# The soft threshold of the later batches on ScalarE and GpSimd instead of VectorE

## The chip, the cores and the metric

The kernel runs on one core of a Trainium2 chip. The metric is the device time of one execution in microseconds (us). Engines are named as in the profile: PE is TensorE's matmul stream and PEld its weight loads, DVE is VectorE, ACT is ScalarE, POOL is GpSimd, SP is the engine that issues most DMAs.

## The reference, cut to what matters

```python
batch, seq, dim = (8, 3008, 256)
X = np.fft.rfft(x, axis=1)
Yr = Xr @ w_r - Xi @ w_i + b_r
Yi = Xr @ w_i + Xi @ w_r + b_i
lam = 0.01
Yr = np.sign(Yr) * np.maximum(np.abs(Yr) - lam, 0.0)
Yi = np.sign(Yi) * np.maximum(np.abs(Yi) - lam, 0.0)
y = np.fft.irfft(Yr + 1j * Yi, n=seq, axis=1)          # (8, 3008, 256)
h = y.reshape(24064, 256) @ w_in                       # w_in: 256 x 2048
out = np.maximum(h, 0.0) ** 2 @ w_out                  # w_out: 2048 x 256
```

Each batch goes through a Fourier transform along the sequence, a complex linear layer, a soft threshold with lam = 0.01, the inverse transform, and a two-layer network with a squared relu.

## The kernel before, in words

**The network** is nearly all of the PE's work. A tile of 500 or 504 tokens (six tiles a batch, 48 in all) meets 8 blocks of the hidden layer; each meeting is a `Step`. Its first layer is made of seven products in PSUM tiles `psh` (left factor `win`, right factor `yt`), three matmuls each, since every number is carried as a high and a low part. DVE adds them up and takes the relu (`mp`, `mu`, `mv`, `mc`), ACT squares `mc` and rounds the square to its high part `mg`, POOL subtracts to get the low part, also `mg`, and 12 matmuls into `pso` (with `wout`) follow two half steps later. A step is done in two slots of the main loop, so a batch has 96 slots. The helper `then` (L486) fixes the order of these instructions on each engine.

**The transform** of the next batch is done beside it. This text calls that a round: in round 1 the network works on the first batch and the transform of the second is made, and so on to round 7, which makes the eighth batch. (The first batch's own transform comes before all that, in a front part of some 150 us with another code, `Unit32`, which the change leaves alone.) In a round, the 24 groups of frequencies are worked off as 12 pairs, `Pair`. A pair runs through these methods: `fwd` makes the second half of the transform (L284, into a PSUM tile `psf`); ACT copies a part (`kq`) and rounds (`kxh`), DVE subtracts (`kxl`) and adds (`kp`); `sums` rounds `kp` on ACT and subtracts on POOL (`kxl` again); `mix` makes two of the three products of the complex layer (L305, 12 matmuls into one `psf`), and DVE adds the bias (`ke`, L317). `shrink` makes the third product (L305, 6 matmuls into another `psf`), DVE combines all in four additions of 64 partitions (`kv`, L326), and then comes the threshold: v minus v clipped to plus or minus lam (L328, L329). ACT rounds the result to `ksh`, POOL subtracts to `ksl`. `back` (L337) runs the inverse, six matmuls for each group of the pair into one `psf` each, four with `ksh` and two with `ksl` in a pair; ACT rounds the outcome (`kuh`), DVE subtracts (`kul`), and both go out by DMA. Other users of `psf` are `Fwd.run` (L240, read by ACT into `xe`) and `Back.mm` (L465 to L469, read by ACT into `dy` and by DVE into `yr`). `Tokens` makes the next tile's `yt` on ACT and POOL from `yr` and `ms`.

All `psf` tiles share two banks of PSUM, in turn: the tile after next has to wait until the bank's readers are done.

**What sets the order.** The main loop emits the methods by due times (in `pair_tasks`, for example, `shrink` comes 4.0 slots after `fwd`, and `back(0)` 7.1 slots after it). A scheduler, which runs a timeline of its own when the kernel is built, then orders all instructions on each engine; at run time each engine takes its own in that order, and an instruction that waits holds up those behind it.

## Time and profile before

| | |
|---|---|
| median of 3 runs | 2633.39 us (2633.01 to 2635.26) |
| profiled execution | 2629.59 us |
| its span, first to last instruction | 2627.5 us |
| PE, DVE, ACT, POOL busy in it | 98%, 68%, 50%, 63% |
| granted TensorE clock | 0.994 |

PE is nearly always busy, so what matters is the small rest: where PE waits, and for whom. Rounds 2 to 6 look alike in the trace, each about 318 us long.

### The profile page before, as it was taken

How to read it: one execution, taken by the hardware profiler on the slowest of the kernel's cores; microseconds unless marked ns; L12 is line 12 of the kernel's file. 1: busy time of each engine (PE TensorE's matmuls, PEld its weight loads, DVE VectorE, ACT ScalarE, POOL GpSimd, SP SyncE). 2: the span in 40 equal slices, each digit the busy share in tenths (PEclk: the TensorE clock that was granted, in tenths of full speed). 3: DMA queues.
4: the chain of work that ended last, by engine and by line, in shares of the span. 5: the costliest groups of instructions: out<-in, count | busy, mean ns of one | idle time of the engine just before them, and what ended most of it. 6: DMA issues, size and time to landing. Idle time of an engine off the chain costs nothing.

```text
span 2627.5 us, 47126 instructions
## 1 busy us (share of the span) xinstructions
PE 2568.5 (98%) x16908; PEld 2348.4 (89%) x16908; DVE 1775.4 (68%) x3797; ACT 1305.1 (50%) x2050; POOL 1655.1 (63%) x1635
## 2 busy tenths in 40 slices
PE   6899999999999999999999999999999999999999
PEld 4789989999899998999989998999989999899998
DVE  7887775666766767566676666666666677665554
ACT  3555445454554545545545444555445454445443
POOL 2356667666766667667666676676667665666564
PEclk8999999999999999999999999999999999999999
DMA  8733333233332333233332333323332222211000
GB/s 267 248 105 107 94 115 93 87 104 103 93 89 88 102 103 87 89 106 98 99 92 81 100 101 104 99 76 98 104 104 83 69 85 80 83 57 47 27 29 16
DMA packets 191066, 250.47 MB, mean 95 GB/s; under 512 B 21790, under 2 KB 135958, under 8 KB 190834
## 3 DMA queue, kind: packets, MB, share of 16 engines
q1 hardware_dynamic: 177970, 223.40, 27.7%
q0 software_dynamic: 12864, 24.07, 4.1%
q8 instruction: 135, 2.21, 0.4%
q14 instruction: 97, 0.79, 0.1%
HBM read 146.85 MB, written 100.53 MB: 94 GB/s over the span
## 4 chain that ended last, share of the span: by engine, by line
PE 88%; DVE 5%; DMA 2%; POOL 2%; issue 1%; ACT 0%; SPq 0%; POOLq 0%; DVEq 0%; ACTq 0%
PE pso L488 38%; PE psh L488 34%; PE psf L305 6%; PE psf L284 2%; PE psf L240 2%; PE psf L337 2%; PE psf L468 1%; PE psf L469 1%; DMA xt<-x_in 1%; PE psf L465 1%; POOL mg L105 1%; DVE kc L328 1%; DVE kv L105 0%; DMA s<-xe 0%; DMA x<-x_in 0%
## 5 line engine op out<-in xcount | busy, mean ns | idle before, releaser
L105 POOL TENSOR_TENSOR mg<-mc,mg 128x500 fp32r<-128x500 f32 (+1 forms) x768 | 965.0, 1277 | 602.6 <-ACT mg L98 542.2
L488 PE MATMUL pso<-mg,wout 128*128 128x500 f32 (+1 forms) x4608 | 1159.4, 392 | 0.4 <-ACT mg L98 0.2
L488 PE MATMUL psh<-yt,win 128*128 128x250 f32 (+1 forms) x8064 | 1077.6, 281 | 3.2 <-DVE mc L102 3.2
L488 PEld LDWEIGHTS psh<-yt,win 128*128 128x128 f32 x8064 | 1020.8, 189 | 33.1 <-PE psh L488 2.7
L488 PEld LDWEIGHTS pso<-mg,wout 128*128 128x128 f32 x4608 | 826.2, 189 | 135.0 <-ACT mg L98 0.7
L102 DVE CUSTOM_DVE_ANT_0 mc<-psh,mv 128x500 f32<-128x500 f32 (+3 forms) x768 | 419.2, 548 | 412.6 <-PE psh L488 370.0
L488 ACT ACTIVATE mc<-mc 128x1000 f32<-128x1000 f32 (+1 forms) x384 | 400.8, 1044 | 478.3 <-DVE mc L102 477.3
L98 ACT CAST mg<-mc 128x1000 fp32r<-128x1000 f32 (+1 forms) x384 | 396.8, 1033 | 18.5 <-ACT mc L488 0.4
L488 DVE TENSOR_TENSOR mv<-psh,mu 128x500 f32<-128x500 f32 (+1 forms) x384 | 260.6, 679 | 51.4 <-PE psh L488 19.3
L305 PE MATMUL psf<-wx,kxh 128*128 128x256 f32 x1008 | 207.5, 282 | 2.7 <-ACT xe L98 1.3
L99 DVE COPY mp<-psh 128x250 f32<-128x250 f32 (+1 forms) x384 | 160.1, 417 | 48.9 <-PE psh L488 27.1
L326 DVE TENSOR_TENSOR kv<-psf,ke 64x256 f32<-64x256 f32 x336 | 141.9, 422 | 57.6 <-PE psf L305 50.3
L305 PEld LDWEIGHTS psf<-wx,kxh 128*128 128x128 f32 x1008 | 165.3, 188 | 6.4 <-ACT xe L98 1.5
L488 DVE TENSOR_TENSOR mu<-psh,mp 128x250 f32<-128x250 f32 (+1 forms) x384 | 160.6, 418 | 11.2
L105 POOL TENSOR_TENSOR ksl<-kv,ksh 128x512 fp32r<-128x512 f32 x84 | 108.7, 1295 | 89.3 <-ACT ksh L98 88.5
L102 DVE CUSTOM_DVE_ANT_0 mc<-psh,mp 128x250 f32<-128x250 f32 (+1 forms) x384 | 157.2, 409 | 1.8 <-PE psh L488 1.4
L98 ACT COPY dy<-psf 128x188 f32<-128x188 f32 x256 | 77.0, 314 | 151.0 <-PE psf L469 149.9
L219 POOL TENSOR_TENSOR xs<-xt 120x256 f32<-120x256 f32 x156 | 116.5, 764 | 50.4 <-DMA xt<-x_in 38.5
L305 PE MATMUL psf<-wx,kxl 128*128 128x256 f32 x504 | 141.1, 280 | 3.5 <-POOL kxl L105 2.8
L98 ACT CAST kuh<-psf 128x256 fp32r<-128x256 f32 x192 | 68.2, 372 | 124.2 <-PE psf L337 107.6
L475 DVE TENSOR_TENSOR yr<-psf,dy 128x188 f32<-128x188 f32 (+4 forms) x256 | 78.3, 313 | 74.5 <-ACT dy L98 68.4
L317 DVE TENSOR_TENSOR ke<-psf,bias 128x512 f32<-128x512 f32 x84 | 58.1, 692 | 100.8 <-PE psf L305 100.3
(103 smaller groups left out, 2531.4 us busy)
## 6 DMA issues: line engine op xcount, KB each, us to landing
du<-s SPq DMA_DIRECT2D x128, 256.0 KB, 2.9
s<-kuh SPq DMA_DIRECT2D x192, 128.0 KB, 2.1
s<-kul SPq DMA_DIRECT2D x192, 128.0 KB, 2.6
ka<-s SPq DMA_DIRECT2D x84, 256.0 KB, 3.4
kcm<-cm_in POOLq DMA_DIRECT2D x84, 256.0 KB, 3.5
s<-xe SPq DMA_DIRECT2D x85, 240.0 KB, 2.4
xt<-x_in SPq DMA_DIRECT2D x84, 240.0 KB, 3.5
du<-s SPq DMA_DIRECT2D x256, 64.0 KB, 2.8
```

The costliest lines, as they stand in the source:

```text
L98: return act.copy(out=out, in_=in_)
L99: return eng.tensor_copy(out=out, in_=in_)
L102: return dve._custom_dve(TENSOR_ADD_SAT, out=out, in0=in0, in1=in1, s0=_float(0x7F7FFFFF), s1=0.0)
L105: return eng.tensor_tensor(out=out, in0=a, in1=b, op=ALU.subtract)
L219: return eng.tensor_tensor(out=out[:, :n], in0=self.xt[:, :n, 0], in1=self.xt[:, :n, 1], op=(ALU.add, ALU.subtract)[t])
L240: nc.tensor.matmul(ps[:M1, t], am32[:, t], self.u[:, t], start=True, stop=True)
L284: nc.tensor.matmul(pv[:, :, c, g, :], self.a[:, g, c * 128:(c + 1) * 128], bg, start=True, stop=True)
L305: self.last = nc.tensor.matmul(ps, l, wx[j][:, k, c, :], start=n == 0, stop=n == 5)
L317: dve.tensor_add(out=self.e, in0=self.pe, in1=bias)
L326: dve.tensor_add(out=v[64 * r:64 * r + 64, g], in0=ps[gs], in1=self.e[gs, r])
L475: self.cut = dve.tensor_add(out=o, in0=ps[:, 0, lo:hi], in1=y[:, c, lo:hi])
L488: last_of[eng] = op(*args, **kwargs)
```

## The change

The threshold of `Pair.shrink` is made as relu(v - lam) - relu(-v - lam). Both relus run on ACT (with a bias that is read from a small tile `low`, filled once with -lam), the subtraction runs on POOL. The clip and the subtraction on DVE go. It concerns 84 pairs, 12 in each of 7 rounds.

```diff
@@ fnet_moe
+    low = const.tile([128, 1], F32, name="low")
...
     nc.sync.dma_start(am32, a32)
+    dve.memset(low, -LAM)
@@ Pair.shrink
                 for r in range(2):
                     dve.tensor_add(out=v[64 * r:64 * r + 64, g], in0=ps[gs], in1=self.e[gs, r])
-            cl = T("kc", [128, 2, D], F32, tag="ke")
-            dve.tensor_scalar(out=cl, in0=v, scalar1=-LAM, scalar2=LAM, op0=ALU.max, op1=ALU.min)
-            sub(dve, v, v, cl)
+            r = T("kc", [128, 2, D], F32, tag="ke")
+            act.activation(r, v, AF.Relu, bias=low)
+            act.activation(v, v, AF.Relu, bias=low, scale=-1.0)
+            sub(pool, v, r, v)
             self.sh = T("ksh", [128, 2, D], F32R)
             self.sl = T("ksl", [128, 2, D], F32R)
             halves(self.sh, self.sl, v, pool)
```

Since the scheduler orders everything anew, the change also moves instructions that the diff does not touch. Up to the first pair of round 1 the order is the same; from there it differs on every engine. Rounds 4 and 6 of the new order are alike, and nearly like round 2; rounds 3 and 5 are alike. Three places show what moved. In the changed kernel a line's number is 1 to 3 higher than before (L284 is L286, L305 is L307, L337 is L340, L488 is L491).

**Place 1: PE, the ninth pair of a round.** Before, in round 4, the first half of this pair's `back` stands inside a run of `pso` matmuls:

```order
L488 MATMUL pso_15737<-mg_16062,wout_83 128x500
L488 MATMUL pso_15737<-mg_16062,wout_84 128x500
L337 MATMUL psf<-ksh,kcm 128x256 x2
L337 MATMUL psf<-ksl,kcm 128x256
L488 MATMUL pso_15738<-mg_16062,wout_83 128x500
L488 MATMUL pso_15738<-mg_16062,wout_84 128x500
```

Now, in the same round:

```order
L468 MATMUL psf<-dx_sb,du 128x2x94
L471 MATMUL psf<-dx_sb,du 128x2x94
L472 MATMUL psf<-dx_sb,du 128x188
L491 MATMUL psh_16286<-yt_16019,win_81 128x250
L286 MATMUL psf<-kb,ka 128x2x64 x4
L340 MATMUL psf<-ksh,kcm 128x256 x4
L491 MATMUL psh_16286<-yt_16018,win_81 128x250
L491 MATMUL psh_16286<-yt_16018,win_82 128x250
L340 MATMUL psf<-ksl,kcm 128x256 x2
L307 MATMUL psf<-wx_79,kxh 128x256
L307 MATMUL psf<-wx_79,kxl 128x256
```

Both halves of `back` now follow the last matmul of `Back.mm` by one `psh` matmul and the next pair's `fwd` (before, `fwd` stood 14 rows ahead of the first `back` row), and the next pair's `mix` follows at once. The two `psh` matmuls between them are the second product of a new tile, which needs the last of the tile's rounded sums (the second `yt<-ms` of place 2).

**Place 2: ACT, the same pair in the same round.** Before:

```order
L98 COPY dy<-psf 128x188
L98 CAST ksh<-kv 128x512
L98 COPY dy<-psf 128x188
L488 ACTIVATE mc<-mc 128x1000
L98 CAST yt_15971<-yr 128x500
L98 COPY kq<-psf 128x256
L98 CAST kxh<-psf 128x512
L98 CAST mg_16138<-mc 128x1000
```

Now:

```order
L331 ACTIVATE kv<-kv,low 128x512
L99 COPY dy<-psf 128x188
L491 ACTIVATE mc<-mc 128x1000
L99 CAST yt_16018<-yr 128x500
L99 COPY kq<-psf 128x256
L99 CAST kxh<-psf 128x512
L99 CAST ksh<-kv 128x512
L99 CAST mg_16254<-mc 128x1000
L99 CAST yt_16018<-ms 128x500
L99 CAST kxh<-kp 128x256
L99 CAST yt_16018<-ms 128x500
```

The rounding `ksh` moved behind five instructions, of which `dy` reads the last matmul of `Back.mm`, and `kq` and `kxh` read the next pair's `fwd`.

**Place 3: PE, the sixth pair of rounds 3 and 5.** Before, its `back` stands among `psh` matmuls (round 3):

```order
L488 MATMUL psh_11336<-yt_10542,win_81 128x250
L337 MATMUL psf<-ksh,kcm 128x256 x2
L337 MATMUL psf<-ksl,kcm 128x256
L337 MATMUL psf<-ksh,kcm 128x256 x2
L337 MATMUL psf<-ksl,kcm 128x256
L488 MATMUL psh_11337<-yt_10541,win_81 128x250
```

Now it stands between `fwd`, a `Fwd.run` and the seventh pair's `mix`, all of which use `psf`:

```order
L491 MATMUL psh_11550<-yt_11293,win_81 128x250
L286 MATMUL psf<-kb,ka 128x2x64 x4
L242 MATMUL psf<-xs,am_76 120x256 x2
L340 MATMUL psf<-ksh,kcm 128x256 x2
L340 MATMUL psf<-ksl,kcm 128x256
L340 MATMUL psf<-ksh,kcm 128x256 x2
L340 MATMUL psf<-ksl,kcm 128x256
L307 MATMUL psf<-wx_79,kxh 128x256
L307 MATMUL psf<-wx_79,kxl 128x256
```

Twelve L307 rows later, after the first of the seventh pair's third product, the eighth pair's `fwd` follows, and after that product a `psh` matmul whose `yt` is rounded on ACT behind that `fwd`'s `kq` and `kxh`.

## The prediction

> **What bounds the kernel now.** I read the page first, then the waits of PE, then the timeline where PE waits.

> ```profile
> PE 2568.5 (98%) x16908; PEld 2348.4 (89%) x16908; DVE 1775.4 (68%) x3797; ACT 1305.1 (50%) x2050; POOL 1655.1 (63%) x1635
> ```

> PE is the bound; ACT and POOL have room on average, so moving work to them can only count where PE waits for its result. The waits of PE (us in total, times, longest) that have to do with the pairs:

> ```profile
> PE psf L337 <- ACT ksh L98: 11.3, 6, 4.0
> PE psh L488 <- DVE mc L102: 3.2, 6, 1.3
> PE psf L305 <- POOL kxl L105: 2.8, 5, 1.0
> ```

> Together 17.3 us, 0.7% of the span. Six of 84 thresholds come late for `back` (L337): the tenth pair of rounds 2 to 6, and one in round 7. The one in round 3, in the timeline (start, duration, engine, instruction, idle time before it and its releaser):

> ```profile
> 997.91 2.48 POOL L105 TENSOR_TENSOR mg<-mc,mg 128x500 fp32r<-128x500 f32 x2
> 998.43 2.95 DVE L328 TENSOR_SCALAR kc<-kv 128x512 f32<-128x512 f32 x1
> 1000.36 0.73 POOL L219 TENSOR_TENSOR xs<-xt 120x256 f32<-120x256 f32 x1
> 1002.46 0.62 ACT L98 CAST ksh<-kv 128x512 fp32r<-128x512 f32 x1 [4.45 <-DVE kv L105]
> 1003.13 0.85 PE L337 MATMUL psf<-ksh,kcm 128*128 128x256 f32 x4 [1.45 <-ACT ksh L98]
> ```

> The clip on DVE lasts 2.95 us and ends when POOL's unbroken run of subtractions ends, at 1001.1. Alone it takes a seventh of that (min, median, max in ns):

> ```profile
> L328 DVE TENSOR_SCALAR kc<-kv x84: 416/566/3304, 187.2 to 2305.4; 128x512 f32<-128x512 f32 x84
> ```

> So what the old threshold costs is a stretched clip that makes `ksh` late, and DVE's `mc` behind it.

> **What the change removes and adds on the engines.**

> ```profile
> L328 DVE TENSOR_SCALAR kc<-kv 128x512 f32<-128x512 f32 x84 | 75.0, 893 | 1.3
> L105 DVE TENSOR_TENSOR kv<-kv,kc 128x512 f32<-128x512 f32 x84 | 67.3, 801 | 0.6
> L105 POOL TENSOR_TENSOR ksl<-kv,ksh 128x512 fp32r<-128x512 f32 x84 | 108.7, 1295 | 89.3 <-ACT ksh L98 88.5
> L152 ACT ACTIVATE da<-dst 128x512 f32<-128x512 f32 x16 | 10.9, 686 | 0.7 <-DMA dst<-w_in_in 0.7
> ```

> DVE loses 75.0 + 67.3 = 142 us. POOL gets 84 subtractions of the size of `ksl`, 84 x 1.295 = 109 us. A relu with a bias from SBUF is not in the trace; the nearest row is the Abs, 0.686 (strided input), with 0.37 (`kq`, half as wide) below and 1.04 (a square of 1000) above as bounds. I take 0.69, so ACT gets 168 x 0.69 = 116 us. All of this is hidden in itself. On a pair's way the minimum grows from 0.42 + 0.68 to 2 x 0.69 + 1.29, by about 1.6 us, and it now passes two more queues. The fill of `low` is one small instruction in the front part: nothing.

> **Term 1, what goes: 17.3 us.** No instruction on DVE between `kv` and `ksh` is left to be stretched, so I take out all three waits, although the 2.8 on `kxl` (POOL's backlog) may stay. Range 11 to 17.3.

> **Term 2, what comes.** The new order puts `back` closer to other users of the two `psf` banks (places 1 and 3). I went through the PE's order of both kernels and compared, for each user of a bank and the next user of the same bank, the PE work between them with the time the readers need. PE's pace, from the chain of waits:

> ```profile
> 749.56 2.45 PE psh L488 x21
> 734.32 2.71 PE pso L488 x12
> 721.30 2.04 PE psf L305 x18
> 726.52 0.86 PE psf L240 x4
> 706.91 0.89 PE psf L284 x8
> ```

> That is 0.117 for a `psh`, 0.226 for a `pso`, 0.113 for L305 and L337, 0.43 for a row of L240, 0.22 for a row of L284 (two matmuls a row in each). The readers:

> ```profile
> L305 PE MATMUL psf<-wx,kxh 128*128 128x256 f32 x1008 | 207.5, 282 | 2.7 <-ACT xe L98 1.3 <-ACT kxh L98 0.7 <-DVE ke L317 0.6
> L98 ACT COPY kq<-psf 128x256 f32<-128x256 f32 x84 | 30.9, 368 | 73.6 <-PE psf L284 73.6
> L98 ACT CAST kxh<-psf 128x512 fp32r<-128x512 f32 x84 | 49.8, 593 | 0.0
> L105 DVE TENSOR_TENSOR kxl<-psf,kxh 128x512 fp32r<-128x512 f32 x84 | 57.7, 686 | 29.0 <-ACT kxh L98 27.6 <-PE psf L468 0.3
> L295 DVE TENSOR_TENSOR kp<-psf,kq 128x256 f32<-128x256 f32 x84 | 34.8, 415 | 0.0
> L98 ACT CAST kuh<-psf 128x256 fp32r<-128x256 f32 x192 | 68.2, 372 | 124.2 <-PE psf L337 107.6 <-DMA s<-kuh 7.5 <-PE psf L430 4.3
> L105 DVE TENSOR_TENSOR kul<-psf,kuh 128x256 fp32r<-128x256 f32 x170 | 69.6, 418 | 29.8 <-ACT kuh L98 27.9 <-issue 0.4
> L317 DVE TENSOR_TENSOR ke<-psf,bias 128x512 f32<-128x512 f32 x84 | 58.1, 692 | 100.8 <-PE psf L305 100.3
> L326 DVE TENSOR_TENSOR kv<-psf,ke 64x256 f32<-64x256 f32 x336 | 141.9, 422 | 57.6 <-PE psf L305 50.3 <-PE psh L488 0.5
> ```

> With 0.28 until a matmul's result is there, a bank is free again 0.28 + 0.37 + 0.59 + 0.69 + 0.42 = 2.35 after `fwd` (2.25, since starts overlap a little), 0.28 + 0.37 + 0.42 = 1.1 after half a `back`, 0.28 + 0.69 = 1.0 after `mix`, 0.28 + 4 x 0.42 = 2.0 after the third product. Before, no next user in rounds 2 to 6 comes earlier than that. Where one does, at the end of round 1, PE does wait (for `xe`, and for a bank, shown as "issue"), and the shortfalls there, 3.1 us, are less than the waits, some 5.8, since queues add to them:

> ```profile
> 350.91 0.39 PE L305 MATMUL psf<-wx,kxh 128*128 128x256 f32 x1 [1.27 <-ACT xe L98]
> 353.81 1.13 PE L284 MATMUL psf<-kb,ka 128*128 128x128 f32 x8 [1.55 <-issue]
> ```

> In the new order every round has such places.

> *Rounds 2, 4 and 6, ninth pair (places 1 and 2).* `ksh` stands behind `dy`, a square, a `yt`, `kq` and `kxh`. The old kernel has nearly that sequence in round 3, without `ksh` at its end:

> ```profile
> 984.85 0.27 PE L469 MATMUL psf<-dx_sb,du 128*128 128x188 f32 x1
> 985.16 0.32 ACT L98 COPY dy<-psf 128x188 f32<-128x188 f32 x1 [0.65 <-PE psf L469]
> 986.04 1.04 ACT L488 ACTIVATE mc<-mc 128x1000 f32<-128x1000 f32 x1 [0.56 <-DVE mc L102]
> 986.98 0.59 ACT L98 CAST yt<-yr 128x500 fp32r<-128x500 f32 x1
> 987.48 0.36 ACT L98 COPY kq<-psf 128x256 f32<-128x256 f32 x1
> 987.75 0.59 ACT L98 CAST kxh<-psf 128x512 fp32r<-128x512 f32 x1
> 988.22 1.04 ACT L98 CAST mg<-mc 128x1000 fp32r<-128x1000 f32 x1
> 989.15 0.62 ACT L98 CAST yt<-ms 128x500 fp32r<-128x500 f32 x1
> 989.66 0.41 ACT L98 CAST kxh<-kp 128x256 fp32r<-128x256 f32 x1
> ```

> From the matmul at 984.85 to the slot behind `kxh` at 988.22 are 3.37; without the square's wait of 0.56, 2.8; plus `ksh`, 0.62 (row above): 3.4. PE comes to `back` after one L469, one `psh` and four rows of L284, 0.11 + 0.12 + 0.89 = 1.1. It waits 2.3 (2.9 with the square's wait). Then four L337, 0.45, and the `psh` that needs the second `yt<-ms`, which ends four ACT instructions after `ksh`: 0.93 + 0.51 + 0.31 + 0.6 = 2.4 later. Another 1.9. Then `mix` needs the bank of `back`'s first half, 1.1 after a matmul that is 0.23 away: 0.85. Sum 5.1 a round; by the banks alone 1.8 + 0.87 = 2.7.

> *Rounds 3 and 5 (place 3).* `back` comes 1.1 after `fwd` where 2.25 are needed: 1.15. `mix` after `back`: 0.7. The eighth pair's `fwd` 0.2 after `mix` where 1.0 is needed: 0.8. The `psh` behind it needs a `yt` whose rounding follows `kq` and `kxh`: 1.6 after `fwd`, with 0.57 of PE work between: 1.0; and its low part on POOL 1.1 later, with 0.23 between: 0.9. In the tenth pair, `mix` after `back`: 0.65. Sum 5.2; banks alone 3.2.

> *Single places.* Round 1: L240 straight after a third product, 1.9. Round 2: `mix` after `back` 0.9, L240 after `mix` 0.8, `fwd` after a third product 1.65: 3.3. Rounds 4 and 6: `mix` after `back` 0.9 each. Round 7: 0.9 + 0.8, and `ksl` late by about 1.0 in the tenth pair: 2.6.

> Sum: 1.9 + (5.1 + 3.3) + 5.2 + 6.0 + 5.2 + 6.0 + 2.6 = 35.3. From below, banks alone: 23. From above, the ratio of waits to shortfalls at the end of round 1, 5.8 / 3.1, times 23: 43.

> **The sum.** 35.3 - 17.3 = +18.0. The profiled execution took 2629.6 (span 2627.5 and 2.1 around it), so it would take 2647.6; its time is 3.8 below the median of the runs, 2633.4, to which the range and the forecast refer: **2651 us**. The ends: 23 - 17.3 = +6, 2639; 43 - 11 = +32, 2665.

> **Rivals.** *Faster: the stretched clip goes and nothing comes.* For it: DVE gets 142 us back, and ACT and POOL are idle half and a third of the time. Against it: the places above are on PE's own order, where idle time elsewhere does not help. 2633.4 - 17.3 = 2616; with a third of the new waits, 2628. Chance 0.11.

> *No change: the waits relieve one another.* A wait gives the queues time, so the one behind it shrinks; if half of 35.3 is left, it equals the 17.3. 2634. Against it: I have counted the waits of one place one after the other already, and most places are far apart. Chance 0.14.

> *Much slower: the longer way is late in every pair.* It decides where the distance from `kv` to `back` is used up. Per pair the work grows from 0.893 + 0.801 to 2 x 0.69 + 1.295, by 0.98; times 84, 82 us: 2715. For it: two more queues, each with instructions of 1.0 to 1.3 us. Against it: only 6 of 84 waits before, and the order gives most pairs more PE work in between than they had (counted at the pace above, mostly 9 to 11 us from the third product to `back`, for 7 to 9). Chance 0.03. [...]

> My forecast has the rest, 0.72.

> **How the numbers follow.** This kernel's measurement tells about 0.2% (5 us) from no change. The forecast's own range, 2639 to 2665, lies above 2638.7, so slower has 0.72 + 0.03 = 0.75, no change 0.14, faster 0.11. For the range I go down to 2636 to take in part of the no-change case, and leave out the faster one and the much slower one.

> **What would show it.** Right: PE's waits at L340 for `ksh` are not gone but come at the ninth pair of rounds 2, 4 and 6, about 2 us each, and at the tenth no more; L307 waits for `kul` or "issue" after `back`, `psh` for `yt`; POOL's runs no longer stretch anything on DVE. PE's idle time in rounds 2 to 7 grows by some 15 us. Wrong: L340 waits for nothing, or rounds 3 and 5 become shorter than 318 us (they should grow by about 2), or the new waits are on POOL's late `mg` or `kv` in many pairs.

## The result, and the profile after

The changed kernel takes **2679.81 us** (median; 2677.4 to 2683.98) against 2633.63 for the kernel before on the same chip, a ratio of 1.0176 (95% interval 1.0158 to 1.0194). It is slower, as forecast, but by 46 us instead of 18, and so outside the range. Its profiled execution took 2680.5 us, span 2678.7, at a granted clock of 0.984 (before 0.994). In the experiments below one execution (of run 6) took 6089.84 us at a full granted clock, a slow state that its figures leave out.

The page of the changed kernel, first the busy times, then the group of the new subtraction:

```profile
PE 2597.0 (97%) x16908; PEld 2368.1 (88%) x16908; DVE 1653.0 (62%) x3630; ACT 1409.8 (53%) x2218; POOL 1746.1 (65%) x1719
...
L106 POOL TENSOR_TENSOR kv<-kc,kv 128x512 f32<-128x512 f32 x84 | 108.5, 1291 | 101.0 <-ACT kv L331 76.9
```

The group of the first relu (the second has 60.7 us in all and a mean of 723 ns):

```profile
L330 ACT ACTIVATE kc<-kv,low 128x512 f32<-128x512 f32 x84 | 60.9, 725 | 102.7 <-DVE kv L328 102.3
```

DVE lost 122 us, ACT and POOL got 105 and 91, and none of the three is near the bound. PE does the same 16908 matmuls, yet is busy 28.5 us longer: its instructions themselves became slower. The waits of PE in the changed kernel (us in total, times, longest), the larger ones that have to do with the pairs:

```profile
PE psf L307 <- DVE kul L106: 11.7, 11, 1.8
...
PE psf L340 <- ACT ksh L99: 6.3, 3, 2.1
...
PE psh L491 <- ACT yt L99: 5.6, 5, 1.7
PE psh L491 <- POOL yt L106: 5.4, 6, 2.2
...
PE psf L340 <- ACT mg L99: 3.6, 2, 2.0
...
PE psf L340 <- POOL ksl L106: 2.4, 5, 1.2
...
PE psf L286 <- DVE ke L319: 1.8, 3, 0.7
```

These are in the main the waits of the prediction. The three on `ksh` are the ninth pairs of rounds 2, 4 and 6; no `ksh` is late at a tenth pair any more. The one of round 4 in the timeline of the changed kernel (start, duration, engine, instruction, idle time before it):

```profile
1338.67 0.37 ACT L99 COPY kq<-psf 128x256 f32<-128x256 f32 x1
1338.93 0.60 ACT L99 CAST kxh<-psf 128x512 fp32r<-128x512 f32 x1
1339.41 0.64 ACT L99 CAST ksh<-kv 128x512 fp32r<-128x512 f32 x1
...
1340.10 1.10 PE L340 MATMUL psf<-ksh,kcm 128*128 128x256 f32 x4 [2.09 <-ACT ksh L99]
...
1341.95 0.61 ACT L99 CAST yt<-ms 128x500 fp32r<-128x500 f32 x1 [0.17 <-POOL ms L106]
...
1342.61 0.79 PE L491 MATMUL psh<-yt,win 128*128 128x250 f32 x2 [1.41 <-ACT yt L99]
...
1344.70 0.58 PE L307 MATMUL psf<-wx,kxh 128*128 128x256 f32 x1 [0.71 <-DVE kul L106]
1345.08 0.41 PE L307 MATMUL psf<-wx,kxl 128*128 128x256 f32 x1
```

The order of events is the one of the prediction: `ksh` behind `kq` and `kxh`, PE waiting at `back`, then at the `psh` for the second `yt<-ms`, then at `mix` for the bank. The new thing is the last row. An L307 matmul elsewhere lasts 0.28 in these records; here it lasts 0.41, and the next starts 0.21 after it instead of 0.11. The same stretch in windows of 3.41 us (window, length, busy us of PE, PEld, DVE, ACT, POOL with their instructions, granted clock, DMA share, GB/s):

```profile
1335.56:1338.97 3.41, 2.45 (x22) 2.26 (x20) 1.42 (x4) 1.95 (x5) 3.41 (x5) 1.00 0.00 0
1338.97:1342.39 3.42, 0.97 (x4) 0.59 (x4) 1.02 (x2) 3.25 (x7) 3.34 (x5) 1.00 0.64 187
1342.39:1345.80 3.41, 2.48 (x9) 2.10 (x10) 0.75 (x2) 0.82 (x3) 3.41 (x4) 0.50 0.18 63
1345.80:1349.21 3.41, 3.41 (x14) 3.01 (x14) 0.69 (x1) 0.00 (x0) 3.34 (x5) 0.50 0.26 91
1349.21:1352.63 3.42, 3.42 (x23) 3.11 (x22) 2.38 (x6) 1.31 (x2) 1.44 (x2) 1.00 0.58 153
```

After the window in which PE was busy for only 0.97 us, its clock is granted at half for two windows, and in the second it does 14 instructions in a full window where it then does 23.

**Where the 51 us of span went.** I took the starts of all matmuls in both traces and called a wait what goes beyond the usual distance of such a pair of rows at the clock of that moment (only waits above 0.25 us). In rounds 2 to 7 (366 to 2335 us) the waits are 20.4 us before and 45.3 after. In the same stretch the clock is granted at 0.50 for 10.2 us before and 51.4 after, which costs half of that: 5.1 and 25.7. So 24.9 + 20.6 = 45.5. The second term is an upper figure: for part of that time at half clock (some 7.6 us after, 2.2 before) PE waited anyway, so the half clock's share is nearer 18. A further 10.2 us at half clock ahead of round 2 (after waits for the first batch's data and at the end of round 1) cost 5.1, and waits there about 1. Together 51.6, or some 49 with the smaller share.

### The profile page after: what moved, and what is told of

It is laid out like the page before. It is cut to its first block, busy times and chain, and to the rows that moved or that the text cites. A ratio compares the mean times of both kernels' runs of the same rounds, so it can differ in the third digit from the quotient of the medians.

```text
span 2678.7 us, 47217 instructions
## 1 busy us (share of the span) xinstructions
PE 2597.0 (97%) x16908; PEld 2368.1 (88%) x16908; DVE 1653.0 (62%) x3630; ACT 1409.8 (53%) x2218; POOL 1746.1 (65%) x1719
## 4 chain that ended last, share of the span: by engine, by line
PE 86%; POOL 5%; DVE 4%; DMA 2%; ACT 2%; issue 1%; SPq 0%; POOLq 0%; ACTq 0%; DVEq 0%
PE pso L491 37%; PE psh L491 32%; PE psf L307 6%; PE psf L242 2%; PE psf L286 2%; PE psf L340 2%; POOL mg L106 2%; PE psf L471 1%; PE psf L472 1%; PE psf L422 1%; PE psf L468 1%; POOL ms L106 1%; DMA xt<-x_in 1%; POOL yt L106 1%; POOL kv L106 1%
## 5 line engine op out<-in xcount | busy, mean ns | idle before, releaser
L491 PE MATMUL pso<-mg,wout 128*128 128x500 f32 (+1 forms) x4608 | 1155.6, 392 | 0.4 <-ACT mg L99 0.2
L491 PE MATMUL psh<-yt,win 128*128 128x250 f32 (+1 forms) x8064 | 1079.1, 281 | 12.5 <-ACT yt L99 5.6
L491 PEld LDWEIGHTS psh<-yt,win 128*128 128x128 f32 x8064 | 1023.7, 189 | 44.1 <-ACT yt L99 7.1
L491 PEld LDWEIGHTS pso<-mg,wout 128*128 128x128 f32 x4608 | 828.1, 189 | 139.7 <-ACT mg L99 0.6
L491 ACT ACTIVATE mc<-mc 128x1000 f32<-128x1000 f32 (+1 forms) x384 | 400.2, 1042 | 409.5 <-DVE mc L103 408.4
L491 DVE TENSOR_TENSOR mv<-psh,mu 128x500 f32<-128x500 f32 (+1 forms) x384 | 260.8, 679 | 49.3 <-PE psh L491 15.8
L307 PE MATMUL psf<-wx,kxh 128*128 128x256 f32 x1008 | 221.2, 296 | 13.5 <-DVE kul L106 11.7
L307 PEld LDWEIGHTS psf<-wx,kxh 128*128 128x128 f32 x1008 | 175.8, 200 | 20.6 <-DVE kul L106 14.2
L106 POOL TENSOR_TENSOR kv<-kc,kv 128x512 f32<-128x512 f32 x84 | 108.5, 1291 | 101.0 <-ACT kv L331 76.9
L328 DVE TENSOR_TENSOR kv<-psf,ke 64x256 f32<-64x256 f32 x336 | 141.7, 422 | 52.4 <-PE psf L307 42.7
L491 DVE TENSOR_TENSOR mu<-psh,mp 128x250 f32<-128x250 f32 (+1 forms) x384 | 160.7, 419 | 12.3
L307 PE MATMUL psf<-wx,kxl 128*128 128x256 f32 x504 | 147.1, 292 | 0.5 <-DVE kxl L106 0.5
L99 ACT CAST kuh<-psf 128x256 fp32r<-128x256 f32 x192 | 67.3, 372 | 148.8 <-PE psf L340 130.0
L319 DVE TENSOR_TENSOR ke<-psf,bias 128x512 f32<-128x512 f32 x84 | 58.1, 691 | 136.9 <-PE psf L307 136.8
L99 ACT COPY xe<-psf 120x512 f32<-120x512 f32 (+1 forms) x98 | 57.0, 581 | 144.9 <-PE psf L242 113.8
```

The lines of the kernel that those rows point to most:

```text
L99: return act.copy(out=out, in_=in_)
L106: return eng.tensor_tensor(out=out, in0=a, in1=b, op=ALU.subtract)
L307: self.last = nc.tensor.matmul(ps, l, wx[j][:, k, c, :], start=n == 0, stop=n == 5)
L319: dve.tensor_add(out=self.e, in0=self.pe, in1=bias)
L328: dve.tensor_add(out=v[64 * r:64 * r + 64, g], in0=ps[gs], in1=self.e[gs, r])
L491: last_of[eng] = op(*args, **kwargs)
```

## The experiments

Theory A: the new order of PE makes the waits, and where they are long they lower the clock; the work that moved to ACT and POOL costs nothing by itself. Against it stood B (the threshold's new way through two more queues costs the time), C (the clock falls by chance) and, for one run, D (what counts is how far `back` stands behind the threshold). "Shortfall" is the prediction's count on PE's order: the time that the next user of a `psf` bank comes too early, summed. It is 26.8 us in the change and 5.6 before. Ratios compare with the kernel before on the same chip; it took 2632.6 us there for runs 1 to 3, 2629.8 for 4 and 5, and 2633.6 for 6 and the eight-place runs of 7.

**1. The change, with `back` due two slots later.** The due time of `back` is one number in `pair_tasks`. It alters nothing of the work, only the order.

```diff
-                first, step, end = 1.0, 6.1, 7.1
+                first, step, end = 1.0, 6.1, 9.1
```

> The changed kernel with one number altered: from round 2 on, back is due 9.1 slots after fwd instead of 7.1. The work on every engine is that of the change. Counted on PE's order with the lags of the prediction, the shortfalls of the two psf banks after the front part fall from 26.8 us (change) to 5.3 us (before has 5.6). Theory A (the new order puts users of a bank too close; the waits this makes also bring the granted clock to half): 2615 to 2640 us, mean clock 0.992 or more, since PE's waits for kul, ksh and yt go and the stretched clip is gone too. Theory B (the longer way of the threshold over two more queues, and fuller ACT and POOL, cost the time wherever back stands): 2660 to 2685 us. Theory C (the half clock has nothing to do with the waits; it is a matter of chance of the program): fewer waits, about 2655 us, clock still near 0.984.

Measured: 2608.45 us (2607.62 to 2611.82), 0.991 of the kernel before (0.9894 to 0.9927). With the same relus on ACT and the same subtraction on POOL it is 71 us faster than the change and 24 faster than the kernel before. In rounds 2 to 7, 0.5 us of waits are left and no stretch at half clock; the 20.4 + 5.1 = 25.5 us that they cost before are the gain. (Between the two spans, 2627.5 and 2607.2, only 20.3 us of it are left: run 1 loses some 6 us ahead of round 2, with a stretch of 6.8 us at half clock at 357 us that the kernel before does not have.) It is faster than theory A's range, 2615 to 2640. Its windows at two of the places:

```profile
680.00:700.00 20.00, 20.00 (x137) 18.47 (x136) 12.39 (x27) 10.98 (x17) 12.01 (x12) 1.00 0.41 124
1335.00:1355.00 20.00, 20.00 (x141) 18.61 (x140) 12.80 (x29) 10.86 (x18) 16.64 (x19) 1.00 0.25 73
```

B falls: the new way costs nothing where the order leaves room for it.

**2. The kernel before, with `back` due one slot earlier.** This gives the old threshold an order with 47.9 us of shortfalls.

```diff
-                first, step, end = 1.0, 6.1, 7.1
+                first, step, end = 1.0, 6.1, 6.1
```

> The kernel before, threshold on VectorE, with one number altered: from round 2 on, back is due 6.1 slots after fwd instead of 7.1. Counted shortfalls of the psf banks: 47.9 us instead of 5.6. Theory A: much slower than before though the threshold is the old one: 2680 to 2740 us, with half-clock stretches in every round (mean clock 0.975 to 0.985). Theory B: 2630 to 2645 us, since neither engine work nor the way of the threshold has changed. Theory C: waits alone, about 2675 us, clock 0.994.

Measured: 2692.78 us (2691.57 to 2694.28), ratio 1.0228 (1.0213 to 1.0244), with the clip still on DVE, and 81.9 us at half clock. Its waits are at the same kind of place:

```profile
PE psf L337 <- ACT ksh L98: 13.5, 5, 3.3
...
PE psf L337 <- ACT mg L98: 9.5, 5, 1.9
...
PE psh L488 <- POOL yt L105: 6.9, 6, 1.7
```

The slowdown can be had without the change, by order alone.

**3. Each half of the change alone.** The relus on ACT with the subtraction left on DVE:

```diff
-            sub(pool, v, r, v)
+            sub(dve, v, r, v)
```

> One part of the change alone: both relus on ScalarE, but their subtraction on VectorE. GpSimd gets no new work. Counted shortfalls 4.9 us. Theory A: 2615 to 2640 us, clock 0.992 or more. Theory B (ACT's part of the cost, 116 us of new work there and one more queue on the way): 2645 to 2665 us. The subtraction reads two SBUF tiles, as the old one did; if that alone can still be stretched by POOL's runs, some waits at back for ksh stay (up to 2 us each).

And the old clip on DVE with the subtraction on POOL:

```diff
-            sub(dve, v, v, cl)
+            sub(pool, v, v, cl)
```

> The other part alone: the clip stays on VectorE, the subtraction goes to GpSimd. Counted shortfalls 8.1 us, most of them 0.9 at one place a round. Theory A: 2630 to 2650 us, with the stretched clip of the tenth pair still there. Theory B (POOL's part of the cost, 109 us of new work there): 2650 to 2670 us.

Measured: the first 2611.67 us (2610.14 to 2614.01), ratio 0.9921 (0.9906 to 0.9936), with shortfalls of 4.9, again below A's range; the second 2641.42 (2640.34 to 2643.98), ratio 1.0034 (1.0021 to 1.0048), with shortfalls of 8.1. In the second the clip is still on DVE, but less stretched: 56.5 us in all instead of 75.0, the longest 1.9 us instead of 3.3; the stretched clip of the tenth pair was expected to stay, but no `back` waits for `ksh` any more (min, median, max in ns):

```profile
L328 DVE TENSOR_SCALAR kc<-kv x84: 417/428/1887, 189.4 to 2321.3; 128x512 f32<-128x512 f32 x84
```

So neither half makes the change's 46 us; the order that each gets goes with its time. That the second is a little slower although the longest stretches are gone fits: it has new waits (5.5 us at L305 for `kul`, 7.5 at `psh` for `yt`), and in rounds 2 to 7 17.1 us at half clock instead of 10.2.

**4. The change, with `back` due three slots later.**

```diff
-                first, step, end = 1.0, 6.1, 7.1
+                first, step, end = 1.0, 6.1, 10.1
```

> The changed kernel with back due 10.1 slots after fwd (change: 7.1, e1: 9.1). Counted shortfalls 19.0 us, between those of e1 (5.3, 2608 us) and of the change (26.8, 2680 us), none above 1.5 at one place in rounds 2 to 7. Theory A by the line through these two, 3.3 us for 1 us of shortfall: 2653 us; less, about 2630, if the waits stay under 2 us each and the clock stays up. Theory D (it is the distance from the threshold to back that counts, not the banks): 2608 us or less, since this distance is longer still.

Measured: 2635.43 us (2632.69 to 2639.15), ratio 1.002 (1.001 to 1.0031). `back` is still farther from the threshold than in run 1, and it is 27 us slower: D falls. The shortfalls are back (19.0), now each below 1.5 us, and a cluster of short waits stands once in each round (L286 for "issue" 9.7 us in 7, L307 for `kxh` 6.1 in 6). The straight line through the first two runs of the change (3.3 us for each us of shortfall) would give 2653; with short waits there is less. The clock did not stay up, though: in the profiled execution (2639.15 us) four of the clusters, whose longest wait is about 1.5 us, still bring 6.8 us at half clock each, 27.3 in all.

**5. Run 1, with the end of round 1 changed too.** Run 1 keeps a cluster of waits at 352 to 361 us. This moves the last `back` there one slot forward:

```diff
-                first, step, end = 11.2, 5.3, 9.1
+                first, step, end = 11.2, 5.3, 8.1
```

> e1 with one more number: in round 1 back is due 8.1 slots after fwd instead of 9.1. Counted shortfalls 3.6 us instead of 5.3, none above 1.0. Theory A: 2600 to 2608 us, and the half-clock stretch at about 357 us, which follows the waits at the end of round 1, is gone. Theory D: slower than e1, since round 1's back comes earlier.

Measured: 2613.46 us (2611.97 to 2618.77), ratio 0.9941 (0.9926 to 0.9957). A miss: the counted shortfalls fell (3.6), but other waits came in their place, 2.1 us at a `psh` for `yt` among them, which the count of banks does not see. The stretch at half clock is not gone but comes at 364 us, 3.4 us long instead of 6.8. Run 1 stays the fastest version.

**6. The kernel before, with the same later `back` as run 1.** Is it the later `back` that helps, with either threshold?

```diff
-                first, step, end = 1.0, 6.1, 7.1
+                first, step, end = 1.0, 6.1, 9.1
```

> The kernel before with back due 9.1 slots after fwd, as in the first run of the change. Counted on PE's order the shortfalls at the psf banks are 23.9 us (5.6 in the kernel before, 5.3 in the change with the later back), none over 1.55, in threes of 0.8, 0.7 and 1.4 once a round. Theory A (the order's spacing of bank users sets the time, and which engine makes the threshold does not): slower than before, 2640 to 2665 us, with waits at those places once a round. Rival (the later back helps by itself, with either threshold): 2606 to 2615 us.

Measured: 2656.56 us (2656.33 to 2660.29), ratio 1.0091 (1.0075 to 1.0108). So at 7.1 slots the old threshold is 46 us faster than the new, and at 9.1 it is some 48 us slower. In rounds 2 to 7 there are 38.7 us of waits and 23.9 us at half clock; 38.7 + 12.0 is 25.2 above the 25.5 of the kernel before, of the 27.3 us between the spans of the two traces; the rest lies ahead of round 2. But the largest waits were not among the counted ones. The timeline of this kernel in round 3:

```profile
1007.59 2.45 POOL L105 TENSOR_TENSOR mg<-mc,mg 128x500 fp32r<-128x500 f32 x2
...
1009.05 2.30 DVE L328 TENSOR_SCALAR kc<-kv 128x512 f32<-128x512 f32 x1
...
1011.38 0.69 DVE L105 TENSOR_TENSOR kxl<-psf,kxh 128x512 fp32r<-128x512 f32 x1
...
1012.12 0.29 PEld L305 LDWEIGHTS psf<-wx,kxl 128*128 128x128 f32 x1 [2.81 <-DVE kxl L105]
```

The clip stands on DVE ahead of the next pair's `kxl` and is stretched beside POOL's subtractions (of the 84 clips here, each of the 42 that last over 0.6 us overlaps POOL's TENSOR_TENSOR instructions for more than half of its time), so PE's weight load waits 2.8 us for `kxl`; this comes once in each of rounds 2 to 6. So A is right that the order sets the time, but not that the engine never matters: the clip on DVE has a harm of its own, which the new threshold takes away.

**7. What a wait costs.** To run 1 I added idle work: reductions of a constant on DVE, 0.69 us each, ahead of DVE's sums at some steps of the last batch's network, where no transform runs beside it. They leave the output as it is. First 16 places with 2 to 8 reductions:

```diff
+            for _ in range(DOSE.get((self.t, self.n), 0)):
+                then(dve, lambda: dve.tensor_reduce(out=zero, in_=bias.rearrange("p j d -> p (j d)"), op=ALU.max, axis=mybir.AxisListType.X))
```

> The kernel of e1, with idle work on VectorE in 16 places of the last batch's network, where no transform runs beside it: before the copy of the first product, 2 to 8 reductions of 512 elements (an estimated 0.6 us each, from the 512-element rows of the trace), so that PE waits at the next product for its bank, about 0 to 4 us. Theory A (a wait of PE that is long enough brings the granted clock to half): half-clock stretches of 3.4 us or more begin at the places with the longest waits and nowhere else in that part; from the waits seen so far the limit lies near 2 us. Theory C (the clock falls by chance or by something else than PE's waits): no relation to the size of the wait, or no half clock in that part, as in all kernels run so far. The time itself is only the sum of the waits: 2608 + 20 to 40.

Measured: 2624.82 us, in a single execution. Waits of 0.64, 0.66, 0.73 and 1.47 us left the clock at 1.00; the two that were longer, 3.10 and 2.17, were each followed by 3.4 us at half.

Then eight places, 17 us apart, with eight reductions each, and the same with six:

```diff
+DOSE = {(45, 0): 8, (45, 3): 8, (45, 6): 8, (46, 1): 8, (46, 4): 8, (46, 7): 8, (47, 2): 8, (47, 5): 8}
```

> The changed kernel with the later back (2608.5 us), and eight reductions of 0.69 us on VectorE ahead of the sums at 8 steps of the last batch's network, 17 us apart, where no transform of a next batch is made. Eight reductions made PE wait 2.17 us at one such step in the run with waits of several sizes. Theory A (a wait of about 2 us costs its length, and in some 15 of 21 cases 3.4 us at half clock, 1.7 us more): 8 x 2.2 = 17.4, and 8 x 0.71 x 1.7 = 9.7, together 27: 2636 us, in a range of 2628 to 2640, with four to eight new half-clock stretches after 2480 us. Rival (a wait costs its length and no more, and the low clock is chance): 2626 us, and no more stretches than the 4 of the kernel without the reductions.

> The same with six reductions at each of the 8 steps. Six made waits of about 0.7 us before. Theory A: eight waits of 0.7 to 1.3, and no half clock: 2608.5 + 6 to 10 = 2614 to 2619 us. If every wait lowers the clock, whatever its length, 8 x 1.7 = 14 come on top: 2628 to 2633 us.

Measured: with eight 2643.1 us (2641.74 to 2646.32), ratio 1.0039 (1.0024 to 1.0053); with six 2621.39 (2620.35 to 2621.91), ratio 0.9953 (0.9938 to 0.9968). The six make PE wait 0.72 and then 0.66 us at nearly every place, 11.4 us more than run 1 has there, and no clock falls: +12.9 us, a little above A's range. The eight make it wait mostly 2.17 and 0.65, 22.0 us more, and seven stretches at half clock, 23.9 us, cost 11.9: together 33.9, measured +34.7. I expected 27 (and at most 2640 us), since I had not seen the second wait at each place. That a wait costs its length only (2626) is excluded, and with it C; so is that every wait lowers the clock. The last 160 us of work of run 1, of the long waits and of the short ones:

```profile
2440.00:2600.00 160.00, 159.80 (x1021) 144.91 (x1020) 91.46 (x192) 75.08 (x86) 93.01 (x85) 1.00 0.06 20
```

```profile
2440.00:2600.00 160.00, 142.89 (x850) 127.71 (x849) 112.40 (x218) 62.39 (x74) 80.20 (x74) 0.94 0.05 18
```

```profile
2440.00:2600.00 160.00, 151.01 (x951) 135.46 (x950) 115.49 (x228) 68.38 (x80) 87.60 (x80) 1.00 0.05 18
```

## Why the prediction was right and wrong

*What bounds the kernel, and what the work costs on the engines:* right. A relu takes 0.724 us where 0.69 was taken, the subtraction 1.291 where 1.295 was; run 1 shows all of it hidden.

*Term 1, what goes (17.3 us):* right in its mechanism; no `ksh` is late at a tenth pair after the change. By the starts of the matmuls rounds 2 to 7 held 20.4 us of waits, and 10.2 us at half clock, which belonged to the term too: in the windows of the kernel before, the tenth pair of round 2 shows it, and I passed over it.

```profile
680.00:700.00 20.00, 18.17 (x107) 16.21 (x106) 13.14 (x24) 7.44 (x11) 9.54 (x10) 0.91 0.30 93
```

*Term 2, what comes (35.3 us):* places and causes right, the sum too small by a quarter. The ninth pair of round 4 was to wait 2.3 for `ksh`, 1.9 for `yt` and 0.85 for the bank; it waits 2.25, 1.47 and 0.89 (full clock taken as the measure), with 0.6 in two small ones besides. The waits over 0.25 us sum up to 8.4 in round 2 (predicted 8.4), 7.4 and 8.0 in rounds 3 and 5 (5.2 each), 7.6 and 7.5 in rounds 4 and 6 (6.0 each) and 5.6 in round 7 (2.6). That round 2 is hit is luck: the 1.65 ahead of a `fwd` came as 0.2 (L286 at 583.91), and a `mix` after `back` took 1.9 instead of 0.9, with 0.5 before it at `back` for `ksl`. The same 1.9 and 0.5 stand in rounds 4 and 6 (L307 at 1229.10 and 1881.09): ACT comes to `kuh` only behind a square and an `mg`, in round 4 at 1228.22, 0.9 us after `back` has ended. What was missed in rounds 3 and 5 is ACT's queue as well. The readers' times were worked out as if the readers began at once, but a square stands ahead of them. The sixth pair of round 3 in the changed kernel's timeline, where `back` needs the bank that `fwd` had:

```profile
951.74 1.03 ACT L491 ACTIVATE mc<-mc 128x1000 f32<-128x1000 f32 x1
...
952.68 0.35 ACT L99 COPY kq<-psf 128x256 f32<-128x256 f32 x1
...
954.16 0.41 DVE L297 TENSOR_TENSOR kp<-psf,kq 128x256 f32<-128x256 f32 x1
...
954.68 0.48 PE L340 MATMUL psf<-ksh,kcm 128*128 128x256 f32 x2 [1.63 <-ACT mg L99]
```

The last reader, `kp`, ends at 954.57 and PE goes on at once (the profile names ACT's `mg`, which ended at 954.45): 1.8 us late where 1.15 was taken, and 2.1 in round 5. In the same way `mix` in the tenth pair waits 1.3, with a square ahead of `kuh`, where 0.65 was taken. In round 7 the low half of a `yt` on POOL stands behind two `mg` of 2.46 us together, and a `psh` waits 2.4. The 1.9 of round 1 did not come: none of its L242 waits. Waits relieving one another, the no-change rival, hardly occurred.

*The sum, 35.3 - 17.3 = +18.0:* this is the step that failed. It priced a wait at its own length. The waits grew by 24.9 us instead of 18.0; the other half, 20.6 us in rounds 2 to 7 and 5.1 ahead of them, is TensorE at half clock after them (upper figures, as said above), a term that the sum did not have. Of the 51 us between the two spans, 18 were forecast, some 7 were mis-sized waits, and 23 to 26 were the missing term. The upper end of the range held only longer waits, so it could not reach there.

*The rivals:* the faster one (2616, nothing comes) is what run 1 reached at 2608, with a different due time. The much slower one had a mechanism, a longer way that is late in every pair, that run 1 refutes: 84 longer ways and no wait. That the subtraction takes 1.291 us on POOL and 0.68 undisturbed on DVE (at 1001.75 in the kernel before) did not decide the outcome: run 1, with it on POOL, takes 2608 us, and the first of run 3, with it on DVE, 2612.

*What would show it:* the waits at L340, L307 and L491 are as said, POOL stretches no threshold on DVE any more. PE's idle time in rounds 2 to 7 was to grow by 15 and grew by 24.9.

## What to carry to other kernels

Where one engine is the bound and each engine takes its work in a fixed order, as in this kernel, moving a small operation can cost what the new order does to the bound engine, and hardly what the operation does to the engines that it joins; try the new placement with a due time or two before judging it, since here the verdict turned from 46 us slower to 24 us faster with one number. When a sum of TensorE's waits is made, look at the granted clock behind each of them: in rounds 2 to 7 of the changed kernel ten windows of 3.41 us in which PE was idle for 1.59 to 2.44 us were each followed by 3.41 to 10.24 us at half clock, which cost up to half of that, and the sum did not have it. A row of windows with the granted clock across the known waits tells this before the change is made.

## What the runs showed of the hardware

Taken in windows of 3.41 us in step with these stretches, PE's idle time in a window is its length less the busy time of PE. After 380 us the changed kernel has ten stretches at half clock, and in the window just ahead of each PE was idle for 1.59 to 2.44 us; of the windows at full clock that full clock followed, none held more than 1.48. In the kernel before, the windows ahead of its two stretches held 1.62 and 1.84 us, and those that full clock followed 1.47 at most. Earlier in the two executions this is less clear: one window with 1.47 us (at 123.0 in the kernel before) was followed by half clock, one with 1.55 (at 351.7 there) and one with 1.76 (at 123.9 in the changed kernel) were not.

The run with the long waits has two places, at the same distance from their steps, each with 2.2 us of wait, that came out differently:

```profile
2537.31:2540.73 3.42, 1.69 (x12) 1.52 (x13) 3.12 (x7) 0.61 (x1) 1.87 (x3) 0.99 0.21 82
2540.73:2544.14 3.41, 3.41 (x11) 2.76 (x10) 1.97 (x5) 2.58 (x3) 2.99 (x4) 0.51 0.00 0
...
2554.38:2557.79 3.41, 2.16 (x14) 1.77 (x13) 3.27 (x6) 0.00 (x0) 2.42 (x2) 1.00 0.00 0
2557.79:2561.21 3.42, 2.18 (x14) 1.96 (x15) 3.01 (x7) 0.41 (x1) 0.00 (x0) 1.00 0.00 0
2561.21:2564.62 3.41, 3.41 (x21) 3.02 (x20) 1.83 (x5) 1.67 (x2) 1.59 (x2) 1.00 0.00 0
```

At the first PE is idle for 1.73 us in one window, and the next is at half clock; at the second the idle time is split over two windows, 1.25 and 1.24, and the clock stays at 1.00. In the kernel before, the waits at the tenth pairs of rounds 2 to 6 left 1.62, 1.45, 1.45, 1.30 and 1.47 us idle in a window, and only the first was followed by half clock.

Left open: what lies behind these stretches, since the runs show no more than the idle time ahead of them and the granted clock; and why the scheduler, given a threshold on other engines, brings `back` next to the other users of the banks.
